# A second Fourier batch and two normalizations emitted beside the feed-forward tail, with four shared row buffers and attention sums made in place

## The chip, the core and the metric

One core of a Trainium2 chip runs the whole kernel in one launch. The metric is device time in microseconds (us). The kernel is written against a framework that owns semaphores, buffer slots and instruction order: the program *emits* instructions, each with a priority that follows the order of emission, and a planner with its own cost model then fixes one order per engine. On the chip each engine takes its instructions strictly in that order. So a line emitted later can be placed earlier by the planner if a slot and its inputs seem ready, but what happens on the chip then waits in the planner's order.

Engines: PE (TensorE, matmuls), DVE (VectorE), ACT (ScalarE), POOL (GpSimd, which also issues some DMAs), SP (issues DMAs only).

## The reference, cut to what matters

```
attn = softmax over scores q k^T / 8, only scores >= max - tau kept     # B=4, H=8, S=576, 64 per head
x    = attn @ v                                    # rows of 512
xk, xr = mixes of x and x shifted by one row (mu_k, mu_r)
x    = sigmoid(xr @ w_r) * (relu(xk @ w_k)**2 @ w_v)                    # "feed-forward", FF = 1024
X    = real(fft over rows of fft over columns)(x);   u = x + X
un   = (u - mean) / sqrt(var + 1e-6)               # per row
out  = u + relu(un @ w_ch1) @ w_ch2                # 512 -> 2048 -> 512
```

Everything is float32 in and out; matmuls use a rounded high part and a remainder (three products for each).

## The kernel before, in words

**Attention** (up to about 597 us) runs over 16 pairs of heads. `emit_av` (line 382) makes one half of a pair's output in a PSUM bank; its `post` copies the other 64 partitions to a scratch tile `avt` (one buffer, pool `at`) on ACT and adds the own half on DVE (line 401), or, for one of the four halves of a pair (bits in `AO`, `AO0`), copies both on ACT and adds on POOL (lines 398, 399). The feed-forward stream (`ffn_stream`, line 451) starts beside the second half of attention.

**Feed-forward tail** (597 to 699 us). The stream goes by batch and half: eight `kps` groups, then the previous half's transposes `xn` (`xt_out`, line 537), four `rps` groups, four `vps` groups. Each `xn` bank is copied by ACT to a tile `xnat` (line 546, one buffer in pool `ffn`) and sent to DRAM (`xd`) by a DMA that ACT issues.

**Fourier part.** For batch b: `fft_fold` (line 850) loads rows (`xa`, `xb`: one buffer each; `ra`, `rb`: tag `o` of pool `chp`, two buffers) and folds them; `fft_one` makes `G` and `H` on PE (tiles `f`, PSUM pool `pst`, two banks); `fft_two` makes `fz`, `fa` (also `pst`) and `fb`, and `make_u` adds and stores two groups `ud[2b]`, `ud[2b+1]`. Nine groups of 256 rows follow: two for each batch, and group 8 from `fft_last`.

**Normalization and mixer.** `norm(g)` loads a group (tile `un`, tag `o` as well) and normalizes it; `turn(g)` transposes it on PE (tile `ut` in the same two banks of `pst`) and copies it to `uts[g]`, a tile of pool `uta`. `uta` lies in the memory of the feed-forward pools, which `fstackp.close()` (line 1045) frees. `mixer` (line 988) then makes 36 steps (q, g), q a quarter of the weights: first q 0 and 1 for groups 0 to 3, then q 0 and 1 for groups 4 to 8, then q 2 and 3. A step has 48 `ch1` matmuls, and 24 `ch2` matmuls that run in the next step and are added by DVE to a tile `u` loaded from `ud`. `quarter(q)` converts a quarter's weights in 16 pieces (`weight_pieces`, line 45): three DVE operations (lines 67 to 69), one ACT copy, one POOL subtraction (line 73).

**What sets the order around the change.** In the loop at line 1027 each step of the stream is followed by 0.6 steps of the chain `side`. In the mixer loop at line 1059 each of a step's four yields takes 2 items of the chain `behind` up to step (0, 3), later 1.25. The last item, `done`, closes the Fourier pools and opens the later `utp`, `lnp` and `ubp` in their memory. `ahead_of` says at which mixer step `norm` and `turn` of a group are emitted.

Of the kernel before, what the change touches and what calls it, by code (L numbers as in the profile page):

```python
# [9 lines left out]
F32 = mybir.dt.float32  # L10
F32R = mybir.dt.float32r
I32 = mybir.dt.int32
ALU = mybir.AluOpType
AF = mybir.ActivationFunctionType
# [5 lines left out]
D, FF, FC = 512, 1024, 2048  # L20
HS = S // 2
NPAIR = H // 2
# [6 lines left out]
def tile_kernel(ctx: ExitStack, tc: tile.TileContext, a):  # L29
# [352 lines left out]
    def emit_av(pi, j, half):  # L382
        ps = bank([128, HS], "av")
        v, u, r = vts[pi], ptu[pi, j, half], ptr[pi, half]
        for k in range(4):
            for x in range(2):
                pe.matmul(ps, v[:, 4 * j + k, :], u[:, x, k, :], start=(k == 0 and x == 0), stop=False)  # L387
        for x in range(2):
            pe.matmul(ps, v[:, 8 + j, :], r[:, x, :], start=False, stop=(x == 1))

        def post():
            b, pr = divmod(pi, NPAIR)
            x = xunit(pi, half)
            own, oth = slice(64 * j, 64 * j + 64), slice(64 - 64 * j, 128 - 64 * j)
            tmp = at.tile([128, HS], F32, tag="avt", name="avt")
            act.activation(tmp[own], ps[oth], AF.Copy)
            if P['AO' if pi >= NPAIR else 'AO0'] >> (2 * half + j) & 1:
                act.activation(x[own, 1:], ps[own], AF.Copy)
                pool.tensor_tensor(x[own, 1:], x[own, 1:], tmp[own], op=ALU.add)
            else:  # L400
                dve.tensor_tensor(x[own, 1:], ps[own], tmp[own], op=ALU.add)
            if j == 1 and half == 1:
                dve.tensor_copy(x[:, 0:1], xT[b, pr, 0][:, HS:HS + 1])
                xdone[1] += 1
            if j == 1 and half == 0:
                xdone[0] += 1

        pending.append(post)
# [13 lines left out]
    def build_xs(b, half, which):  # L422
        fp = ffn["pool"]
        hi = fp.tile([128, 4, HS], F32R, tag="xh", name="xh")
        lo = fp.tile([128, 4, HS], F32R, tag="xl", name="xl")

        def chunk(c):
            x = xT[b, c, half]
            tmp = fp.tile([128, HS], F32, tag="xtmp", bufs=2, name="xtmp")
            m = 4 * which + c  # L430
            if P['XD'] >> (4 * which + c) & 1:
                act.activation(tmp, x[:, 0:HS], AF.Copy, scale=mus[:, 8 + m:9 + m])
                t = lo[:, c, :].bitcast(F32)
                act.activation(t, x[:, 1:], AF.Copy, scale=mus[:, m:m + 1])
                pool.tensor_tensor(tmp, t, tmp, op=ALU.add)
                act.activation(hi[:, c, :], tmp, AF.Copy)
                pool.tensor_tensor(lo[:, c, :], tmp, hi[:, c, :].bitcast(F32), op=ALU.subtract)
                return
            if b == B - 1 and P['XT'] and half + P['XT'] > 1:
                dve.tensor_scalar(tmp, x[:, 0:HS], mus[:, 8 + m:9 + m], None, op0=ALU.mult)  # L440
            else:
                pool.tensor_scalar(tmp, x[:, 0:HS], mus[:, 8 + m:9 + m], 1.0, op0=ALU.mult, op1=ALU.mult)
            dve.scalar_tensor_tensor(tmp, x[:, 1:], mus[:, m:m + 1], tmp, op0=ALU.mult, op1=ALU.add)
            act.activation(hi[:, c, :], tmp, AF.Copy)
            eng = dve if b == B - 1 and (c < P['XL']) else pool
            eng.tensor_tensor(lo[:, c, :], tmp, hi[:, c, :].bitcast(F32), op=ALU.subtract)

        builds.extend((lambda c=c: chunk(c)) for c in range(4))
        return hi, lo

    def ffn_stream():
        fp = ffn["pool"]
        xt_out = None
        for b in range(B):
            for half in range(2):
# [81 lines left out]
                def xt_out(b=b, half=half, t=t):  # L537
                    settle()
                    for t0 in (0, 128, 256):
                        tn = min(128, HS - t0)  # L540
                        ps = bank([128, D], "xn")
                        for m in range(4):
                            pe.transpose(ps[:tn, 128 * m:128 * (m + 1)], t[:, m, t0:t0 + tn], ident)

                        def post(t0=t0, tn=tn, ps=ps):
                            n = fp.tile([128, D], F32, tag="xn", name="xnat")
                            if P['XN'] >> (t0 // 128) & 1:
                                dve.tensor_scalar(n[:tn], ps[:tn], 0.5, None, op0=ALU.mult)
                            else:
                                act.activation(n[:tn], ps[:tn], AF.Copy, scale=0.5)  # L550
                            r0 = half * (HS + 1) + t0
                            act.dma_start(xd[b][r0:r0 + tn, :], n[:tn])
                            if half and t0 == 256:
                                act.dma_start(xd[b][HS:HS + 1, :], n[tn - 1:tn])

                        pending.append(post)
                        yield 0.45
                    written[b] += 1
# [170 lines left out]

    rstack = ctx.enter_context(ExitStack())  # L730
    chp = rstack.enter_context(tc.tile_pool(name="chp", bufs=1, side="right"))
    stage2 = rstack.enter_context(tc.tile_pool(name="stage2", bufs=1, side="right"))
    fstack, fstack1 = ExitStack(), ExitStack()
    psc = ctx.enter_context(tc.tile_pool(name="psc", bufs=3, space=PSUM))
# [25 lines left out]

    def load_rem(b):

        xa = chp.tile([128, D], F32, tag="o", bufs=2, name="ra")[:98]
        xb = chp.tile([128, D], F32, tag="o", bufs=2, name="rb")[:98]
        for r in (0, 33, 65):
            sp.dma_start(xa[r:r + 32], xd[b][256:288, :])
            sp.dma_start(xb[r:r + 32], xd[b][544:576, :])
        for r in (32, 97):
            sp.dma_start(xa[r:r + 1], xd[b][576:577, :])
            sp.dma_start(xb[r:r + 1], xd[b][576:577, :])  # L770
        return xa, xb
# [78 lines left out]
    def fft_fold(b):  # L850
        while written[b] < 2:
            yield
        settle()
        prs = prs_of[b] = load_pairs(b)
        ra, rb = load_rem(b)
        parts_e, parts_o = [], []
        for xa, xb in prs:
            e, o = folded(xa, xb, 128)
            yield
            parts_e.append(split_tile(e, 257, "fse"))  # L860
            parts_o.append(split_tile(o, 256, "fso"))
            yield
        e, o = folded(ra, rb, 98)
        yield
        ske = stack_tile(e, 257, "ske")
        sko = stack_tile(o, 256, "sko")
        fold_of[b] = (parts_e, parts_o, ske, sko)
        yield
# [30 lines left out]
            yield  # L899

    def fft_last():
        xa = chp.tile([128, D], F32, tag="o", bufs=2, name="xar")
        xb = chp.tile([128, D], F32, tag="o", bufs=2, name="xbr")
        for b in range(B):
            sp.dma_start(xa[32 * b:32 * b + 32], xd[b][256:288, :])
            sp.dma_start(xb[32 * b:32 * b + 32], xd[b][544:576, :])
        gr = [x.rearrange("p c b r -> p c (b r)") for x in grem]
        pa, pb = stage_2(gr[0:2], gr[2:4], 64, 0, 128)
        make_u(8, pa, pb, xa, xb)
        yield  # L910

    def chain(*gens):
        for g in gens:
            yield from g
# [4 lines left out]
    def quarter(q):  # L919

        t = [big(f"{'AB'[q % 2]}{i}", f"c{'AB'[q % 2]}{i}") for i in range(2)]
        wq[q] = t
        todo = []
        for k, src in enumerate(("w_ch1", "w_ch2")):
            to = whole([x[:, 2048 * k:2048 * k + 2048] for x in t], 2048 * q)
            todo += [(a[src], to, j) for j in range(8 * q, 8 * q + 8)]
        yield from weight_pieces(todo, None, stage2, 256, rb=4, bb=2)


    uts, hs = {}, {}  # L930

    def norm(g):

        u = [lnp.tile([128, D], F32, tag="o", bufs=2, name="un") for _ in range(2)]
        for j in range(2):
            sp.dma_start(u[j], ud[g][:, j])
        st = chp.tile([128, 32], F32, tag="lnst", bufs=1, name="lnst")
# [83 lines left out]


    fft_done, utp, lnp, ubp = False, None, chp, None
    side = chain(fft_fold(0), fft_one(0), fft_two(0))
    cgen = None
    acc = 0.0
    for _ in stream:
# [18 lines left out]
    utp = ctx.enter_context(tc.tile_pool(name="uta", bufs=1, side="left"))  # L1046
    hsp = ctx.enter_context(tc.tile_pool(name="hsp", bufs=1, side="left"))
    ubp = ctx.enter_context(tc.tile_pool(name="ub", bufs=1, side="left"))
    turn(0, norm(0))
    for _ in cgen:  # L1050
        pass
    behind = chain(
        fft_fold(1), fft_one(1), fft_two(1), quarter(1), fft_fold(2), fft_one(2), fft_two(2),
        fft_fold(3), fft_one(3), fft_two(3), fft_last(), done(),
    )

    ahead_of = {(0, 0): 1, (0, 1): 2, (0, 2): 3, (1, 2): 4, (1, 3): 5, (0, 5): 6, (0, 6): 7, (0, 7): 8}
    credit = 0.0
    for (q, g), f in mixer():
        credit += 2.0 if (q, g) < (0, 4) else 1.25  # L1060
# [141 lines left out]
```

## Time and profile before

| | us |
|---|---|
| three runs | 1182.55, 1186.1, 1186.32 (median 1186.1) |
| profiled execution | 1183.13 |
| its span, first to last instruction | 1181.4 |
| PE busy | 1054.0 (89%) |
| DVE busy | 812.3 (69%) |
| ACT busy | 596.3 (50%) |
| POOL busy | 501.2 (42%) |

Busy time of PE overlaps itself (matmuls are pipelined), so the count of matmuls in a stretch tells more than the share. A row of the view of stretches gives, for each engine, busy time and (x) the number of instructions, then PE's granted clock as a share of 2.4 GHz.

### The profile page before, as it was taken

To read this page: it belongs to the slowest core of one execution; us is meant where nothing else is said; L and a number is where in the kernel's file an instruction comes from. 1 tells how busy PE (TensorE), PEld (TensorE's weight loads), DVE (VectorE), ACT (ScalarE), POOL (GpSimd) and SP (SyncE) were. 2 spreads that over 40 slices of the span, in tenths; PEclk is the share of its full clock that TensorE was granted. 3 is DMA by queue.
4 is the path that set the end of the run, shared out by engine and by line. 5 is a ranking of instruction groups with operands and counts; after the bars stand their busy time and mean duration, and the time that the engine had idled before them with its cause. 6 is when DMAs were issued, how large, how long until landed. Compare 5 with 4: busy or idle time off the path is not lost.

```text
span 1181.4 us, 20038 instructions
## 1 busy us (share of the span) xinstructions
PE 1054.0 (89%) x7109; PEld 973.5 (82%) x7109; DVE 812.3 (69%) x2077; ACT 596.3 (50%) x1410; POOL 501.2 (42%) x649
## 2 busy tenths in 40 slices
PE   3676678899989999999979769799979999999998
PEld 3665568898989998899979758699869999999997
DVE  7999897977889887888756699536454758322222
ACT  5788777577685866858545724323232213111111
POOL 4566686656466565656442565000001536110000
PEclk9788789999999999999989889899989999999999
DMA  5333320111111111111063255434343555222221
GB/s 170 102 113 116 93 71 32 54 54 42 54 50 56 53 62 35 54 51 42 12 183 118 80 153 164 176 97 143 107 161 107 164 176 165 104 104 93 90 102 59
DMA packets 40395, 114.07 MB, mean 97 GB/s; under 512 B 6191, under 2 KB 6612, under 8 KB 40296
## 3 DMA queue, kind: packets, MB, share of 16 engines
q1 hardware_dynamic: 27200, 74.57, 19.8%
q0 software_dynamic: 10400, 33.50, 8.9%
q10 hardware_dynamic: 2696, 4.73, 1.1%
q8 instruction: 56, 0.92, 0.3%
q14 instruction: 43, 0.35, 0.1%
HBM read 84.45 MB, written 28.32 MB: 95 GB/s over the span
## 4 chain that ended last, share of the span: by engine, by line
PE 66%; DVE 16%; DMA 7%; ACT 5%; issue 4%; POOL 2%; SPq 0%; DVEq 0%; ACTq 0%; POOLq 0%
PE c1ps L972 6%; PE c1ps L971 6%; PE c1ps L973 6%; PE c2ps L984 5%; PE c2ps L985 5%; PE c2ps L986 5%; PE av L387 4%; PE s L212 4%; PE t L320 3%; DMA rawqk<-in_qk 3%; DVE q L167 2%; PE vps L526 2%; PE kps L418 2%; DVE small L252 2%; PE vps L528 2%
## 5 line engine op out<-in xcount | busy, mean ns | idle before, releaser
L977 DVE SCALAR_TENSOR_TENSOR hl<-c1ps,hh 128x256 fp32r<-128x256 f32 x144 | 60.9, 423 | 185.0 <-ACT hh L976 184.3
L976 ACT ACTIVATE hh<-c1ps 128x256 fp32r<-128x256 f32 x144 | 55.2, 383 | 230.6 <-PE c1ps L973 230.1
L1009 POOL DMA_DIRECT2D ud<-u x54 | 29.5, 547 | 255.0 <-DVE u L1008 199.2
L252 DVE TENSOR_REDUCE small<-s 128x1 f32<-128x576 f32 x144 | 106.3, 749 | 15.2 <-PE s L212 12.2
L267 DVE SCALAR_TENSOR_TENSOR e<-s,small,e 128x576 f32<-128x576 f32 x128 | 102.1, 811 | 9.3 <-ACT e L263 7.4
L273 POOL TENSOR_SCALAR e<-e,small 128x576 f32<-128x576 f32 x104 | 82.4, 798 | 43.0 <-DVE small L633 33.7
L263 ACT ACTIVATE e<-s,small 128x576 f32<-128x576 f32 x128 | 92.6, 743 | 12.5 <-DVE small L252 9.1
L320 PE MATMUL t<-ident,e 128*128 128x128 f32 x512 | 84.1, 294 | 15.1 <-DVE ptr L306 6.4
L971 PE MATMUL c1ps<-ut,cA 128*128 128x256 f32 x288 | 83.2, 291 | 14.4 <-ACT ut L962 14.4
L212 PE MATMUL s<-kh,q 128*128 128x288 f32 x256 | 66.0, 342 | 26.1 <-DVE q L167 13.6
L972 PE MATMUL c1ps<-ut,cA 128*128 128x256 f32 x288 | 83.6, 290 | 1.1 <-DVE ut L963 1.1
L306 DVE TENSOR_TENSOR pt<-t,pt 128x512 fp32r<-128x512 f32 x100 | 67.8, 684 | 23.5 <-ACT pt L305 22.9
L973 PE MATMUL c1ps<-ut,cA 128*128 128x256 f32 x288 | 82.9, 288 | 0.0
L320 PEld LDWEIGHTS t<-ident,e 128*128 128x128 f32 x512 | 65.6, 151 | 20.4 <-ACT e L639 6.0
L418 PE MATMUL kps<-xh,wk 128*128 128x288 f32 x256 | 79.3, 310 | 2.2 <-ACT relu L473 1.6
L971 PE MATMUL c1ps<-ut,cB 128*128 128x256 f32 x288 | 81.2, 282 | 0.0
L973 PE MATMUL c1ps<-ut,cB 128*128 128x256 f32 x288 | 81.1, 281 | 0.0
L972 PE MATMUL c1ps<-ut,cB 128*128 128x256 f32 x288 | 81.0, 281 | 0.0
L387 PE MATMUL av<-pt,v 128*128 128x288 f32 x408 | 72.8, 311 | 7.4 <-ACT pt L305 4.0
L488 POOL TENSOR_TENSOR k<-relu,k 128x288 fp32r<-128x288 f32 x64 | 56.7, 887 | 51.6 <-ACT k L486 51.3
L419 PE MATMUL kps<-xl,wk 128*128 128x288 f32 x256 | 77.5, 303 | 0.0
L420 PE MATMUL kps<-xh,wk 128*128 128x288 f32 x256 | 77.2, 302 | 0.0
(243 smaller groups left out, 3607.1 us busy)
## 6 DMA issues: line engine op xcount, KB each, us to landing
rawqk<-in_qk SPq DMA_DIRECT2D x32, 608.0 KB
u<-ud SPq DMA_DIRECT2D x36, 512.0 KB
wraw<-in_w_ch POOLq DMA_DIRECT2D x64, 256.0 KB, 3.0
ud<-u POOLq DMA_DIRECT2D x54, 256.0 KB, 2.5
rawv<-in_v SPq DMA_DIRECT2D x16, 288.0 KB
un<-ud SPq DMA_DIRECT2D x18, 256.0 KB
out<-u SPq DMA_DIRECT2D x18, 256.0 KB
wraw<-in_w_k SPq DMA_DIRECT2D x8, 512.0 KB
```

Of the source, the lines that this page charges most:

```text
L212: pe.matmul(ps[:, h, 0:HS], q[:, c:c + 128], kk[:, h * HS:(h + 1) * HS], start=(x == 0), stop=(x == 1),)
L252: dve.tensor_reduce(st[:, 0:1], sps[n][:, :, 0:HS], axis=AX.XY, op=ALU.max, negate=True)
L263: act.activation(two(eview(n)), sps[n][:, :, 0:HS], AF.Exp, bias=st[:, 0:1])
L267: dve.scalar_tensor_tensor(e, sps[n][:, :, 0:HS], st[:, 1:2], e, op0=ALU.is_ge, op1=ALU.mult, accum_out=st[:, 2:3])
L273: pool.tensor_scalar(e, e, st[:, 2:3], 1.0, op0=ALU.mult, op1=ALU.mult)
L320: pe.transpose(t[:, k, :], e[:, o + 128 * k:o + 128 * (k + 1)], ident)
L387: pe.matmul(ps, v[:, 4 * j + k, :], u[:, x, k, :], start=(k == 0 and x == 0), stop=False)
L418: pe.matmul(ps, wh, x[0][:, k, :], start=(k == 0), stop=False)
L419: pe.matmul(ps, wh, x[1][:, k, :], start=False, stop=False)
L971: pe.matmul(ps, wh, ut[0][:, k, :], start=(k == 0), stop=False)
L972: pe.matmul(ps, wh, ut[1][:, k, :], start=False, stop=False)
L973: pe.matmul(ps, wl, ut[0][:, k, :], start=False, stop=(k == 3))
```

## The change

`emit_av` copies the other half straight into the result tile with ACT and adds in place on DVE, in all cases; `avt` and the POOL form are gone. From the opening of `chp` on, `xnat` is allocated there, with tag `o`, which now has four buffers (also used by `ra`, `rb`, `xar`, `xbr` and, while `norm` uses `chp`, by `un`). The weight stage has three raw buffers in place of four. `side` now also holds batch 1's fold, `norm(0)` and `norm(1)`, and batch 1's two stages. `turn(0)` and `turn(1)` stand together before the mixer. `behind` no longer has batch 1, and groups 2 and 3 are normalized one step earlier.

```diff
@@ emit_av / post
-            tmp = at.tile([128, HS], F32, tag="avt", name="avt")
-            act.activation(tmp[own], ps[oth], AF.Copy)
-            if P['AO' if pi >= NPAIR else 'AO0'] >> (2 * half + j) & 1:
-                act.activation(x[own, 1:], ps[own], AF.Copy)
-                pool.tensor_tensor(x[own, 1:], x[own, 1:], tmp[own], op=ALU.add)
-            else:
-                dve.tensor_tensor(x[own, 1:], ps[own], tmp[own], op=ALU.add)
+            act.activation(x[own, 1:], ps[oth], AF.Copy)
+            dve.tensor_tensor(x[own, 1:], ps[own], x[own, 1:], op=ALU.add)
@@ ffn_stream / xt_out
-                            n = fp.tile([128, D], F32, tag="xn", name="xnat")
+                            n = fp.tile([128, D], F32, tag="xn", name="xnat") if last is None else last.tile([128, D], F32, tag="o", bufs=4, name="xnat")
@@ after chp is opened
+    last = chp
@@ load_rem (and fft_last likewise)
-        xa = chp.tile([128, D], F32, tag="o", bufs=2, name="ra")[:98]
-        xb = chp.tile([128, D], F32, tag="o", bufs=2, name="rb")[:98]
+        xa = chp.tile([128, D], F32, tag="o", bufs=4, name="ra")[:98]
+        xb = chp.tile([128, D], F32, tag="o", bufs=4, name="rb")[:98]
@@ quarter
-        yield from weight_pieces(todo, None, stage2, 256, rb=4, bb=2)
+        yield from weight_pieces(todo, None, stage2, 256, rb=3, bb=2)
@@ norm
-        u = [lnp.tile([128, D], F32, tag="o", bufs=2, name="un") for _ in range(2)]
+        u = [lnp.tile([128, D], F32, tag="o", bufs=4 if lnp is chp else 2, name="un") for _ in range(2)]
@@ before the stream's tail
-    side = chain(fft_fold(0), fft_one(0), fft_two(0))
+    normed = {}
+    def norms():
+        for g in range(2):
+            normed[g] = norm(g)
+            yield
+    side = chain(fft_fold(0), fft_one(0), fft_two(0), fft_fold(1), norms(), fft_one(1), fft_two(1))
@@ before the mixer
-    turn(0, norm(0))
+    for g in range(2):
+        turn(g, normed[g])
     behind = chain(
-        fft_fold(1), fft_one(1), fft_two(1), quarter(1), fft_fold(2), fft_one(2), fft_two(2),
+        quarter(1), fft_fold(2), fft_one(2), fft_two(2),
         fft_fold(3), fft_one(3), fft_two(3), fft_last(), done(),
     )
-    ahead_of = {(0, 0): 1, (0, 1): 2, (0, 2): 3, (1, 2): 4, (1, 3): 5, (0, 5): 6, (0, 6): 7, (0, 7): 8}
+    ahead_of = {(0, 0): 2, (0, 1): 3, (1, 2): 4, (1, 3): 5, (0, 5): 6, (0, 6): 7, (0, 7): 8}
```

## Rows read from the trace of the kernel before

**Rows 1.** Stretches: length, busy (count) of PE, PEld, DVE, ACT, POOL, PEclk, DMA.

```profile
664.00:699.20 35.20, 26.66 (x174) 24.65 (x172) 32.85 (x65) 15.97 (x37) 24.29 (x36) 0.85 0.42 117
...
710.00:753.40 43.40, 36.54 (x228) 31.96 (x229) 35.02 (x86) 16.79 (x47) 17.14 (x27) 0.93 0.62 201
753.40:854.00 100.60, 99.54 (x645) 89.92 (x646) 53.05 (x146) 31.94 (x90) 5.42 (x10) 0.96 0.31 106
...
870.40:1164.00 293.60, 293.58 (x1888) 267.69 (x1889) 130.51 (x282) 60.46 (x151) 58.49 (x94) 0.99 0.34 115
```

**Rows 2.** Timeline of PE: start, length, line, tiles, idle before and its releaser.

```profile
671.07 0.61 PE L418 MATMUL rps<-xh,wr 128*128 128x288 f32 x1 [3.48 <-ACT xnat L550]
...
676.50 0.61 PE L418 MATMUL rps<-xh,wr 128*128 128x288 f32 x1 [2.05 <-ACT xnat L550]
...
698.57 0.61 PE L543 MATMUL xn<-ident,tg 128*32 128x128 f32 x4 [0.25 <-ACT xnat L550]
...
710.04 0.80 PE L971 MATMUL c1ps<-ut,cA 128*128 128x256 f32 x2 [10.87 <-ACT ut L962]
...
749.15 1.36 PE L960 MATMUL ut<-ident,un 128*128 128x128 f32 x8 [3.45 <-ACT un L952]
753.40 0.80 PE L971 MATMUL c1ps<-ut,cA 128*128 128x256 f32 x2 [2.89 <-ACT ut L962]
```

**Rows 3.** Chain that ended last, 697 to 711 us: start, length, what.

```profile
702.37 3.40 DMA xd<-xnat
...
706.46 2.37 DMA xd<-xnat
...
708.91 0.61 ACT ut L962
```

**Rows 4.** Timeline of PE: who holds the two `pst` banks.

```profile
652.47 0.66 PE L960 MATMUL ut<-ident,un 128*128 128x128 f32 x4
...
715.35 0.38 PE L802 MATMUL f<-tc,fseh 128*128 128x290 f32 x1
```

**Rows 5.** DVE groups by line and form, 714 to 742.5 us: count, busy, mean ns.

```profile
L838 DVE TENSOR_TENSOR xa<-xa,fdd 128x257 f32<-128x257 f32 x2 | 0.8, 420 | 0.0
...
L810 DVE TENSOR_TENSOR G<-f,G 128x290 fp32r<-128x290 f32 x2 | 0.9, 446 | 0.0
```

**Rows 6.** Timelines of DVE and POOL: two-input DVE operations with and without POOL's beside them.

```profile
608.05 1.85 DVE L780 TENSOR_TENSOR fy<-fp,fq 128x257 f32<-128x257 f32 x1
...
608.06 1.55 POOL L488 TENSOR_TENSOR k<-relu,k 128x288 fp32r<-128x288 f32 x2
...
683.94 1.22 DVE L69 SCALAR_TENSOR_TENSOR wbits<-wraw,wbits 128x256 int32<-128x256 int32 x1
...
684.12 0.76 POOL L73 TENSOR_TENSOR cA<-wbits,cA 128x256 fp32r<-128x256 f32 x1
...
734.66 0.42 DVE L69 SCALAR_TENSOR_TENSOR wbits<-wraw,wbits 128x256 int32<-128x256 int32 x1
```

**Rows 7.** Timeline of SP: loads of batches 2 and 3, and the first `u` after them.

```profile
745.45 0.80 SPq L757 DMA_DIRECT2D xa<-xd  x2
...
766.71 0.32 SPq L766 DMA_DIRECT2D ra<-xd  x1
...
804.98 0.80 SPq L757 DMA_DIRECT2D xa<-xd  x2
```

**Rows 8.** Chain that ended last, 840 to 872 us.

```profile
853.32 4.92 DMA u<-ud
...
870.42 0.79 PE c1ps L971 x2
```

**Rows 9.** Attention's sums: durations min/median/max of POOL's form; and the first table load.

```profile
L399 POOL TENSOR_TENSOR xt<-xt,avt x16: 792/802/1260, 72.1 to 595.6; 64x288 f32<-64x288 f32 x16
...
597.61 0.74 POOL L746 DMA_DIRECT2D tc<-in_tc  x1 [1.25 <-DVE xt L401]
```

**Rows 10.** The page's DMA issues: KB each, us from issue to landing.

```profile
wraw<-in_w_ch POOLq DMA_DIRECT2D x64, 256.0 KB, 3.0
```

More of the change, by code (lines that the diff above doesn't have):

```diff
@@ L449, in build_xs @@
         return hi, lo
+    last = None
     def ffn_stream():
@@ L901, in fft_last @@
     def fft_last():
-        xa = chp.tile([128, D], F32, tag="o", bufs=2, name="xar")
-        xb = chp.tile([128, D], F32, tag="o", bufs=2, name="xbr")
+        xa = chp.tile([128, D], F32, tag="o", bufs=4, name="xar")
+        xb = chp.tile([128, D], F32, tag="o", bufs=4, name="xbr")
         for b in range(B):
```

## The prediction

> **What bounds the kernel now.** I read first the page's table of 40 slices (attention up to about 597 us, DVE the fullest engine in its first part; then a broken stretch in which PE's clock falls several times; from about 870 us PE full to the end), then a view by stretches, then PE's waits inside the broken stretch, then the chain of waits.
>
> From 870.4 to 1164 us PE does 1888 matmuls in 293.6 us [rows 1]. A mixer step is 48 + 24 = 72 matmuls, so that is 26 steps (1872) and 16 transposes: 293.6 / 26 = 11.3 us a step, with no wait. Step 9 of 36, (0, 5), starts at 870.42 [rows 8]; from there to the end the kernel is bound by PE and the change alters nothing. So the question is only: **when does step 9 start?** Everything earlier in it is gained one for one.
>
> Before that, three holes. (1) The last feed-forward matmuls end at 699.2 (698.57 + 0.61), the first of the mixer starts at 710.04 after 10.87 us of idle [rows 2]. The chain says why: the last `xnat` copies share one buffer, two DMAs of 3.40 and 2.37 us stand in series, and only behind the second does ACT copy `ut`, at 708.91 [rows 3]: `xnat` lies in a pool whose memory `ut` takes over. (2) The same buffer holds PE back by 3.48 and 2.05 us at 671 and 676.5 [rows 2]. (3) PE transposed group 0 at 652.47 already, and those tiles sat in both `pst` banks until ACT could copy them at 708.91; so batch 1's `f` started only at 715.35 [rows 3, 4]. Its 68 matmuls then shared 710 to 753.4 with two mixer steps, and group 2, which needs them, kept PE waiting 3.45 and 2.89 us at 749 and 753 [rows 1, 2].
>
> Behind this stands a second chain, batches 2 and 3. Their buffers are single, so batch 2 loads at 745.45, batch 3 at 804.98 [rows 7], and only when the last store is issued does SP load `u` into the memory that `done` freed: 853.32, landing 4.92 us later; step 9 starts 17.1 us after that load [rows 8]. Before, both chains arrive together at 853.
>
> **The change, part by part.**
>
> *`xnat` in four buffers.* Takes away the serial DMAs: `ut` can be copied when the last transposes are done, 699.2, not 708.91 [rows 2, 3]: -9.7 us. In the tail it takes away 2.05 us; of the 3.48 I count 1, since `xs` of that half is still being built. Sum -3. Against it: `un` of groups 0 and 1 hold up to four `o` buffers, so the third `xnat` of a half can wait until group 0 is transposed. If so ACT stands with it and PE's banks stay full: between 0 and about +10 us; I take 0, since by order of emission two `xnat` stand ahead of `un(1)`, and keep 10 in the range.
>
> *Batch 1's two stages beside the tail.* What really moves is `fft_one(1)` and `fft_two(1)`; the planner had the fold ahead already. PE: 68 matmuls of 256 to 290 columns; a mixer step of 11.3 us streams 48 x 256 + 24 x 512 = 24,576 columns [rows 1], 0.46 ns each, so I estimate 0.125 us a matmul and 8.5 us in all. In 664 to 699.2 PE has 174 matmuls in 35.2 us [rows 1]; at 0.13 us each that is 23 us, so some 12 us are free, 3 of which I have just spent. I charge 4 of the 8.5 to the tail (between 0 and 8.5). DVE: 5 splits of 0.45 and 12 adds of 0.42 us [rows 5] = 7.3 us, in a stretch where DVE is busy 32.85 of 35.2 us [rows 1] with weight pieces. Those are not needed before the mixer reads them, so they slip behind, into the mixer's first steps, where DVE was busy 35.0 of 43.4 us (710 to 753.4). Tail and mixer start: 699.2 - 3 + 4 = 700.2, then one transposition, copy and first matmul, 2 to 3 us: **703** in place of 710.
>
> DVE's two-input operations take 0.42 us with POOL quiet, but 1.22 when POOL's subtraction of 0.76 lies inside, and 1.85 beside two of POOL's of together 1.55 [rows 6]. Eight of the moved adds have two inputs in SBUF, and before they ran with POOL quiet. Between 0 and 8 x 0.76 = 6 us more for DVE; I take 3, as not every add meets one. The Trainium skill (SBUF — State Buffer, "Who interferes with whom") says that a DVE instruction with two SBUF inputs and a GpSimd instruction that reads SBUF exclude each other for the whole instruction; by it all that overlap pay in full, which speaks against this move and would put 6 in place of 3; the trace's 1.85 us agrees.
>
> *The mixer's first nine steps.* 710 to 753.4 held two steps, 8.5 us of batch 1 and 6.3 us of waits for it: 43.4 - 8.5 - 6.3 = 28.6 us. 753.4 to 854 held seven steps with batches 2 and 3 beside them, 100.6 us [rows 1]. PE alone would then start step 9 at 703 + 28.6 + 100.6 = **832**.
>
> *Batches 2 and 3.* `xa` is free when batch 1 is stored: I put its last adds at 695 to 698 and the load at 703, not 745.45 [rows 7]: -42. Batch 2's `ra` waited for an `o` buffer until 766.71 [rows 7], 21 us behind `xa`; with four buffers some 8 us of that go. DVE is fuller at 703 to 745 than at 745 to 790: +7 (between 0 and 15). `u` is loaded at 853.3 - 42 - 8 + 7 = 810.
>
> *An earlier `done`.* `behind` loses 11 items, 51 to 40. Of these 32 are emitted in the first 16 yields, the rest at 1.25: `done` falls on yield 16 + 7 = 23 (step 5), before on 16 + 16 = 32 (step 7). So `u` of step 5, not of step 7, is the first to lie in the freed memory, and PE stands two steps earlier if the batches are late. With 17.1 us from that load to a step's start, as before, it is now step 8 that starts at 810 + 17 = 827, and step 9 at **838**.
>
> *In-place sums.* 16 of POOL's adds of 0.80 us [rows 9] become DVE adds of about 0.46, and 16 ACT copies go. PE is the fuller engine in the later attention; in the early part DVE is, with 4 or 5 of the 16: between -1 and +2, I take 0. The first table load waited for the last reader of `avt` until 597.61 [rows 9]; without `avt` it can go 2 us sooner, which the tail hides.
>
> *Three raw buffers.* With two loads ahead and 3.0 us from issue to landing [rows 10] a piece may go every 1.5 us without waiting for a load; DVE needs 3 x 0.42 = 1.3 us for one, and 0.8 more where POOL's subtraction lies inside [rows 6]: 0. If loads slow down, quarter 1 is late, but is needed only at step 4, near 750.
>
> *Sum.* Step 9 at the later of 832 and 838: 838, so 870.4 - 838 = 32 us gained: span 1181.4 - 32 = 1149, profiled execution 1183.1 - 32 = 1151. The median of the runs shown, 1186.1, is 3 above that execution, and one run lies below it; I add 1: **1152**.
>
> **The rivals.**
>
> *B. Group 0 takes the banks again.* If PE has `ut(0)` in both `pst` banks before `f` of batch 1, as at 652 [rows 4], batch 1 waits for the pool, about 702, and not 715: it runs beside steps 0 and 1. Loads of batch 2 at 735, `u` at 853 - 10 - 8 + 2 = 837, step 9 at 837 + 28 = 865: 1177. For it: the planner did so. Against: `f` is now emitted far ahead of `ut`, and its first input comes with the first half of the fold.
>
> *C. Slower, by the earlier `done`.* If batches 2 and 3 end no sooner than now, PE stands at step 7 waiting for `u`, with the same 17 us behind it: step 9 at 853 + 28 = 881, 11 us late: 1194. It decides from a load of `u` at 842 on (842 + 28 = 870). For it: `quarter(1)` is now emitted ahead of batch 2 and DVE is full there. Against: that needs batch 2 to lose all of 42 us.
>
> *D. The gain is used up.* The tail pays for batch 1 in full (8.5 PE, 13 DVE with `xnat` held): start near 712 and, through late stores, step 9 at 868 to 872: 1183. The change then does not do what it says, since the work stood beside nothing idle.
>
> **How the numbers follow.** Forecast A 0.57 at 1152, on its own from 1138 to 1166: both chains 10 to 14 us better (832 - 8 for PE, `u` at 797), or the 10 of `xnat` and the upper 8 on DVE. B 0.20 at 1177, C 0.12 at 1194, D 0.11 at 1183. A measurement of this kernel tells about 0.3%, 3.6 us: 1182.5 to 1189.7 is no change. Faster: A, 0.17 of B and 0.03 of D: 0.77. Same: 0.03 of B and 0.08 of D: 0.11. Slower: C, 0.12. The range from 1138 to 1182 leaves out C, half of D and a few in a hundred below.
>
> **What would show it.** The idle before the first `c1ps` falls from 10.87 to under 4 us and stands near 700; `f` of batch 1 on PE lies between 650 and 690, ahead of `ut`; no PE wait near 749; `u` loaded into freed memory near 810; step 9 near 838, then 11.3 us a step unchanged. Wrong would be: `ut` ahead of `f`; ACT waiting for an `o` buffer in the tail; PE standing at step 7 for `u` longer than about 10 us; or attention's end moved by more than 3 us.

## The result

The changed kernel takes 1139.1 us (median of four runs, 1136.3 to 1142.4) where the kernel before takes 1184.3 beside it: a ratio of 0.962, 95% interval 0.9585 to 0.9656. The forecast of 1152 had the sign right and a gain too small: 32 us at step 9, where 44.7 came. The time lies at the lower edge of the stated range (1138 to 1182), and one of the four runs below it.

In the profiled execution step 9 starts at 825.7 us in place of 870.4, and the span falls from 1181.4 to 1138.1. The view of stretches of the changed kernel, columns as in [rows 1]: the last 35 us of the feed-forward, mixer steps 0 and 1, steps 2 to 8, steps 9 to 34.

```profile
660.00:695.10 35.10, 29.09 (x202) 25.90 (x200) 29.74 (x80) 19.11 (x46) 16.62 (x26) 0.96 0.53 162
696.60:725.50 28.90, 27.08 (x152) 23.08 (x153) 23.14 (x67) 12.59 (x31) 12.82 (x21) 0.89 0.62 201
725.50:825.70 100.20, 100.20 (x669) 90.47 (x668) 67.94 (x184) 34.58 (x96) 21.55 (x37) 1.00 0.51 170
825.70:1120.80 295.10, 295.10 (x1908) 268.40 (x1907) 132.71 (x276) 59.53 (x151) 59.54 (x98) 1.00 0.36 123
```

From 725.5 on the view shows PE without a gap. Behind step 9 little has changed: 295.1 us for 26 steps, where [rows 1] has 293.6. PE's timeline holds these waits where before had those of [rows 2], and no other over 0.6 us between 665 and 826:

```profile
685.87 0.40 PE L523 MATMUL vps<-k,wv 128*128 128x288 f32 x1 [1.86 <-DVE tg L529]
...
692.89 2.20 PE L540 MATMUL xn<-ident,tg 128*128 128x128 f32 x9 [2.55 <-DVE tg L529]
...
696.62 0.58 PE L969 MATMUL c1ps<-ut,cA 128*128 128x256 f32 x1 [1.54 <-ACT ut L960]
```

The 10.87 us ahead of the mixer are 1.54; the `xnat` waits are gone and waits for DVE's `tg` have taken part of their place. Batch 1's first `f` runs on PE at 643.18 (before 715.35 [rows 4]), ahead of group 0's transposes:

```profile
643.18 0.30 PE L800 MATMUL f<-tc,fseh 128*128 128x290 f32 x1
...
668.38 0.63 PE L958 MATMUL ut<-ident,un 128*128 128x128 f32 x4 [0.53 <-DVE fdd L835]
```

SP's timeline, which answers to [rows 7] and the first row of [rows 8]: batch 2's rows load at 677.69 (before 745.45), and `u` goes into freed memory at 786.46, ahead of the last store of the Fourier part at 803.66:

```profile
677.69 0.80 SPq L755 DMA_DIRECT2D xa<-xd  x2
...
786.46 0.32 SPq L996 DMA_DIRECT2D u<-ud  x1
786.82 0.90 SPq L934 DMA_DIRECT2D un<-ud  x2
...
803.66 0.38 SPq L844 DMA_DIRECT2D ud<-xbr  x1
```

**Where the 44.7 us at step 9 come from**, by the two traces. The attention ends 3.5 us earlier (first `vps` at 592.0 for 595.5). The stretch from there to the last `vps` takes 97.3 us for 100.1: -2.8. From the last `vps` to the last `xn` it takes 5.8 for 3.6: +2.2, the `tg` waits. The idle time ahead of the first mixer matmul: -9.3. Steps 0 to 8: 129.1 for 160.4, -31.3. Sum -44.7; 1.4 of it are lost again behind step 9.

### The profile page after: what moved, and what is told of

The parts are those of the page before. It is cut to its first block, busy times and chain, and to the rows that moved or that the text cites. A ratio compares the mean times of both kernels' runs of the same rounds, so it can differ in the third digit from the quotient of the medians.

```text
span 1138.1 us, 19981 instructions
## 1 busy us (share of the span) xinstructions
PE 1038.4 (91%) x7109; PEld 960.0 (84%) x7109; DVE 806.7 (71%) x2093; ACT 588.9 (52%) x1396; POOL 483.8 (43%) x633
## 4 chain that ended last, share of the span: by engine, by line
PE 65%; DVE 16%; ACT 7%; DMA 6%; issue 4%; POOL 2%; SPq 0%; DVEq 0%; ACTq 0%; POOLq 0%
PE c1ps L969 6%; PE c1ps L971 6%; PE c1ps L970 6%; PE c2ps L984 6%; PE c2ps L982 6%; PE c2ps L983 6%; PE av L387 3%; PE s L212 3%; DVE q L167 3%; DMA rawqk<-in_qk 2%; PE t L320 2%; DVE small L252 2%; PE kps L413 2%; DVE e L267 2%; PE kps L415 2%
## 5 line engine op out<-in xcount | busy, mean ns | idle before, releaser
L267 DVE SCALAR_TENSOR_TENSOR e<-s,small,e 128x576 f32<-128x576 f32 x128 | 102.4, 811 | 7.3 <-ACT e L263 5.6
L320 PE MATMUL t<-ident,e 128*128 128x128 f32 x512 | 81.2, 290 | 7.9 <-DVE ptr L306 2.9
L969 PE MATMUL c1ps<-ut,cA 128*128 128x256 f32 x288 | 82.5, 286 | 2.2 <-ACT ut L960 1.5
L970 PE MATMUL c1ps<-ut,cA 128*128 128x256 f32 x288 | 82.0, 285 | 0.0
L523 PE MATMUL vps<-k,wv 128*128 128x288 f32 x256 | 76.7, 302 | 5.4 <-DVE tg L529 4.6
L971 PE MATMUL c1ps<-ut,cA 128*128 128x256 f32 x288 | 81.6, 283 | 0.0
L485 POOL TENSOR_TENSOR k<-relu,k 128x288 fp32r<-128x288 f32 x64 | 54.1, 847 | 60.6 <-ACT k L483 59.7
L413 PE MATMUL kps<-xh,wk 128*128 128x288 f32 x256 | 78.3, 306 | 0.8 <-ACT relu L470 0.4
L415 PE MATMUL kps<-xh,wk 128*128 128x288 f32 x256 | 75.6, 296 | 0.0
```

What stands on the lines that cost most here:

```text
L267: dve.scalar_tensor_tensor(e, sps[n][:, :, 0:HS], st[:, 1:2], e, op0=ALU.is_ge, op1=ALU.mult, accum_out=st[:, 2:3])
L320: pe.transpose(t[:, k, :], e[:, o + 128 * k:o + 128 * (k + 1)], ident)
L413: pe.matmul(ps, wh, x[0][:, k, :], start=(k == 0), stop=False)
L415: pe.matmul(ps, wl, x[0][:, k, :], start=False, stop=(k == nk - 1))
L969: pe.matmul(ps, wh, ut[0][:, k, :], start=(k == 0), stop=False)
L970: pe.matmul(ps, wh, ut[1][:, k, :], start=False, stop=False)
```

## The experiments

The table has what the sections below speak of: in each profiled execution the start of step 0, step 2 and step 9, the difference of the last two, and the ratio to the kernel before on the same chip.

| kernel | step 0 | step 2 | step 9 | 2 to 9 | ratio (95%) |
|---|---|---|---|---|---|
| before | 710.0 | 753.4 | 870.4 | 117.0 | 1 |
| + four buffers (e8) | 716.7 | 765.6 | 868.0 | 102.4 | 0.9998 (0.9979 to 1.0016) |
| + buffers, group 0 early (e10) | 702.5 | 768.4 | 870.6 | 102.2 | 0.9986 (0.9970 to 1.0002) |
| + buffers, sums (e2) | 708.7 | 757.7 | 858.8 | 101.1 | 0.9910 (0.9883 to 0.9937) |
| + buffers, sums, group 0 early (e9) | 692.1 | 754.6 | 856.0 | 101.4 | 0.9883 (0.9860 to 0.9907) |
| + buffers, sums, groups 0, 1 early (e12) | 690.2 | 746.7 | 850.3 | 103.6 | 0.9875 (0.9854 to 0.9896) |
| changed kernel (a0: again) | 696.6 | 725.5 | 825.7 | 100.2 | 0.9609 (0.9586 to 0.9632) |
| changed, `xnat` alone in its buffer (e1) | 706.3 | 733.6 | 835.6 | 102.0 | 0.9689 (0.9661 to 0.9717) |
| changed, old sums (e3) | 703.2 | 730.1 | 832.4 | 102.3 | 0.9677 (0.9653 to 0.9701) |
| changed, scratch tile, DVE adds (e4) | 707.8 | 735.3 | 835.4 | 100.1 | 0.9727 (0.9712 to 0.9743) |
| changed, `u` over the last tables (e5) | 697.0 | 725.2 | 833.1 | 107.9 | 0.9637 (0.9616 to 0.9658) |
| changed, subtraction on DVE (e6) | 695.2 | 721.6 | 821.7 | 100.1 | 0.9604 (0.9586 to 0.9623) |

**a0: the changed kernel beside the others.**

> The changed kernel itself, on the same chip as the three edits beside it: 1139 us, within 0.3% (1136 to 1143).

1138.6 us (1137.8 to 1140.1). The differences below are from this. The kernels ran on three chips, on which the kernel before took 1182.5 to 1185.1 us, so between chips the ratios of the table decide.

**e1: `xnat` back in its one buffer.**

```diff
- n = last.tile([128, D], F32, tag="o", bufs=4, name="xnat")
+ n = fp.tile([128, D], F32, tag="xn", name="xnat")
```

> The changed kernel with xnat back in its single buffer in the feed-forward pool; all else stays. Theory 1 (from the mixer's start PE is the bound, so a later start is paid one for one): the idle before the first c1ps is again about 10 us, the feed-forward waits of 2 to 4 us come back, and the time is 10 to 13 us longer, 1149 to 1152. Rival (batches 2 and 3 set when step 9 starts, as the prediction had it): the gap comes back but is hidden, 0 to 3 us, 1139 to 1142.

1147.9 us, 9.4 above, a little under the 10 to 13 of Theory 1. The mixer starts 9.7 us later, at 706.3, and from there to step 9 nothing differs (129.3 us for 129.1). In PE's timeline the wait of [rows 2] is back, and in the chain that ended last (start, length, what) the two stores in series of [rows 3]:

```profile
706.30 0.79 PE L969 MATMUL c1ps<-ut,cA 128*128 128x256 f32 x2 [9.50 <-ACT ut L960]
```

```profile
699.25 2.69 DMA xd<-xnat
...
702.64 2.46 DMA xd<-xnat
...
705.17 1.09 ACT ut L960 x2
```

So what `xnat` in the shared buffers is worth in the changed kernel is shown, and it is two of the prediction's terms: the idle ahead of the mixer is 8.0 us longer (9.50 for 1.54; the prediction took 9.7), and the feed-forward from the attention's end to the last `xn` 3.7 longer (106.8 us for 103.1; the prediction took 3). That their sum at the mixer's start is again 9.7 is chance: the attention ended 2.0 us earlier in this run.

**e8: the four buffers alone, in the kernel before** (with three raw weight buffers, as in the change).

```diff
- n = fp.tile([128, D], F32, tag="xn", name="xnat")
+ n = last.tile([128, D], F32, tag="o", bufs=4, name="xnat")   # ra, rb, xar, xbr, un: bufs=4 too
```

> The kernel before with the buffers alone: xnat in chp, four o buffers, three raw buffers. Theory 1: the mixer and batch 1 both start some 10 us earlier and all of it is kept, 1171 to 1175. Rival (batches 2 and 3 hold step 9 at the end of step 8): 1181 to 1184, the earlier start turns into a longer wait near step 8.

1184.5 us: no change. The rival's time came, to half a microsecond, but not its wait near step 8. The stores are no longer waited for; PE's timeline has a longer wait in their place, for the normalized rows of group 0. SP's timeline shows when they were loaded, and SP's waits (who waited for what: us in total, times, longest) what stood ahead of them:

```profile
714.10 1.97 PE L963 MATMUL ut<-ident,un 128*128 128x128 f32 x8 [18.65 <-ACT un L955]
```

```profile
696.00 0.44 SPq L939 DMA_DIRECT2D un<-ud  x1
696.49 0.43 SPq L1001 DMA_DIRECT2D u<-ud  x1
697.48 0.32 SPq L939 DMA_DIRECT2D un<-ud  x1
```

```profile
SPq L1001 <- PE xn L545: 50.9, 1, 50.9
...
SPq L939 <- DMA xd<-xnat: 0.5, 1, 0.5
```

Group 0's `un` stands behind the three `xnat` of the last half in the order of emission, and now in the same four buffers: it is loaded at 696 to 697.5 us, where before it had two buffers without `xnat` and its transposes ran at 652.47 [rows 4]. On SP the first of its two loads stands behind a load of `u`, for which SP waits 50.9 us until the last `xn`; only the second waits for a store of `xnat`, 0.5 us. The buffers are all that differs from the kernel before, so the planner's new order on SP comes of them; how it arrives at that order no run takes apart. In exchange steps 2 to 8 run without the waits that [rows 8] ends in: 102.4 us for 117.0. The mixer starts 6.7 us later and reaches step 2 12.2 later; 14.6 less behind it leave step 9 at 868.0.

**e2: batch 1 and both normalizations late, buffers and sums as changed.**

```diff
- side = chain(fft_fold(0), fft_one(0), fft_two(0), fft_fold(1), norms(), fft_one(1), fft_two(1))
+ side = chain(fft_fold(0), fft_one(0), fft_two(0))
  # turn(0, norm(0)), behind and ahead_of as in the kernel before
```

> The changed kernel with batch 1's fold and stages, norm and turn of groups 0 to 3 emitted where they were; the four shared buffers, the three raw buffers and the sums stay. Theory 1: batch 1's 8.5 us of PE and the waits of some 6 us for group 2 come back into the first steps, and done falls late again: 15 to 28 us longer, 1154 to 1167. Rival (the buffers alone bring the gain): 1139 to 1143.

1174.1 us, 35.5 above, more than Theory 1 asked for: e8's wait is in it, 18.74 us here. In the chain that ended last, group 0's second load comes behind a store of `xnat` and takes 8.86 us:

```profile
686.70 2.70 DMA xd<-xnat
689.47 8.86 DMA un<-ud
```

**e9 and e10: group 0's normalization early, batch 1 late**, in the changed kernel and in e8.

```diff
  def norms():
-     for g in range(2):
-         normed[g] = norm(g)
-         yield
+     normed[0] = norm(0)
+     yield
- side = chain(fft_fold(0), fft_one(0), fft_two(0), fft_fold(1), norms(), fft_one(1), fft_two(1))
+ side = chain(fft_fold(0), fft_one(0), fft_two(0), norms())
```

> The changed kernel with batch 1's transform and group 1's normalization put back to where they were before, but group 0's normalization kept beside the last feed-forward halves. With group 0 also late the time was 1174 us, 35.5 above the changed kernel, and PE waited 18.7 us before the first transposition of group 0, since its load queued behind the stores of the x rows, whose four buffers it shares. Theory 1, of these 35.5 some 16 are that wait, and 15 to 24 are batch 1's work in the first nine steps: mixer start at 689 to 693, steps 0 to 9 in 150 to 158 us as in the two kernels with batch 1 late (150.1 and 151.3), 1154 to 1162. Rival 1, batch 1's place is worth little and nearly all was the wait: 1140 to 1148. Rival 2, the transform of three batches holds step 9 at the same instant however early the mixer starts: step 9 at 856 to 860, 1170 to 1175.

> The kernel before with the x rows in the shared four buffers (as in the run with the buffers alone, 1184.5) and group 0's normalization moved beside the last feed-forward halves; batch 1 stays late, sums as before. Theory 1, the buffers alone gained nothing because they took away 10.9 us ahead of the first mixer product and put in 18.7 ahead of the first transposition, since group 0's load queues behind the x rows in the same buffers; with that normalization early the mixer starts at 696 to 699 (before 710.0), steps 0 to 9 take 151 to 160 us and the time is 1160 to 1172. Rival, the transforms of batches 1 to 3 hold step 9 at 868 to 870 whatever the mixer's start: 1181 to 1186.

1172.7 and 1183.5 us. Theory 1 fell in both. The mixer does start at 692.1 and 702.5, 16.6 and 14.2 us earlier than without the edit, but step 9 moves by 2.8 us, and by 2.6 the wrong way. What the mixer wins at its start it stands at step 2, the first that needs rows of batch 1. The waits in e9, from PE's timeline:

```profile
713.82 1.87 PE L958 MATMUL ut<-ident,un 128*128 128x128 f32 x8 [4.48 <-ACT un L950]
717.14 0.61 PE L800 MATMUL f<-tc,fseh 128*128 128x290 f32 x1 [1.44 <-DVE ut L961]
...
748.52 1.97 PE L958 MATMUL ut<-ident,un 128*128 128x128 f32 x8 [8.48 <-ACT un L950]
754.60 0.80 PE L969 MATMUL c1ps<-ut,cA 128*128 128x256 f32 x2 [4.12 <-ACT ut L960]
```

and its stretches, from the last `xn` to step 2 and from there to step 9:

```profile
689.70:754.60 64.90, 40.91 (x228) 34.52 (x228) 50.53 (x123) 23.06 (x59) 25.42 (x40) 0.84 0.60 194
754.60:856.00 101.40, 100.88 (x655) 90.99 (x656) 56.80 (x160) 34.91 (x97) 5.40 (x10) 0.96 0.38 123
```

24.0 us idle in the first, 0.5 in the second. The rival's time (in e9 the second rival's) was right and its mechanism not quite: not the transforms of three batches hold step 9, but batch 1's holds step 2, and from step 2 on PE is full.

**e12: only batch 1 late**, groups 0 and 1 early.

```diff
- side = chain(fft_fold(0), fft_one(0), fft_two(0), fft_fold(1), norms(), fft_one(1), fft_two(1))
+ side = chain(fft_fold(0), fft_one(0), fft_two(0), norms())
  # behind begins with fft_fold(1), fft_one(1), fft_two(1); ahead_of {(0, 1): 2, (0, 2): 3, ...}
```

> The changed kernel with only batch 1's transform put back behind the mixer's first steps; groups 0 and 1 are both normalized beside the last feed-forward halves (both hold rows of batch 0 only). In the three kernels with batch 1 late whose rows I followed, step 2 comes 37.5 to 38.7 us after the first table product f of batch 1 (before 715.35 to 753.4, with group 0's normalization alone early 717.1 to 754.6, the same with the sums of before 729.7 to 768.4), and step 9 another 101 to 102 us after step 2 where the four buffers are shared. And f stands on PE behind the transposition of group 1, whose rows were loaded only at 698 to 709, behind the x rows in the same buffers. Theory 1: with group 1 early, f follows the mixer's start (about 692) by 0 to 8 us, step 2 comes at 730 to 738, step 9 at 832 to 840 (825.7 in the changed kernel), 1145 to 1153; so most of the 34 us between 1138.6 and 1172.7 are group 1's normalization and not batch 1's place. Rival: batch 1's fold is what is late, f stays at about 717, step 9 at 856, 1168 to 1174.

1167.5 us: a miss. `f` came at 697.46, as Theory 1 said, but step 2 followed 49 us behind it, not 38, at 746.7; PE did steps 0 and 1 and then stood for rows stored at 729.3 to 732.6:

```profile
744.05 1.97 PE L958 MATMUL ut<-ident,un 128*128 128x128 f32 x8 [17.30 <-ACT un L950]
```

So emitting batch 1 early, with all else as changed, is worth 0.9875 - 0.9609 = 0.0266 of 1185, 31 us, and 24.6 us at step 9 in the two profiled executions. But batch 1 is later in e12 than it was in the kernel before. There the planner had put batch 1's fold beside the tail, as the prediction says, and its remainder rows `ra` were loaded at 653.19 us; in e12 they come at 694.17, on SP behind a `u` again, and then behind an `xnat`, whose buffers they share. SP's timeline before and in e12, and SP's waits in e12:

```profile
653.19 1.25 SPq L766 DMA_DIRECT2D ra<-xd  x3
```

```profile
694.17 0.32 SPq L764 DMA_DIRECT2D ra<-xd  x1
```

```profile
SPq L996 <- PE xn L540: 52.5, 1, 52.5
SPq L764 <- DMA xd<-xnat: 4.8, 1, 4.8
```

In e8, e2, e9 and e10 `ra` comes as late, at 690 to 702 us. So with the four buffers the late batch 1 comes later still, and its early emission takes that back too; no run prices the two apart, and why step 2 followed `f` by 49 us in place of 38 wasn't isolated. Between the last `xn` and step 2 PE stands idle 21.4 us here, 24.0 in e9, 17.7 in the kernel before (54.2 less 36.5) and 3.3 in the changed kernel (30.4 less 27.1, 695.1 to 725.5). Whether e12 and e9 differ the intervals don't tell.

**e3 and e4: the attention's sums.** e3 has the old ones, e4 the scratch tile with DVE doing every addition.

```diff
- act.activation(x[own, 1:], ps[oth], AF.Copy)
- dve.tensor_tensor(x[own, 1:], ps[own], x[own, 1:], op=ALU.add)
+ tmp = at.tile([128, HS], F32, tag="avt", name="avt")
+ act.activation(tmp[own], ps[oth], AF.Copy)
+ dve.tensor_tensor(x[own, 1:], ps[own], tmp[own], op=ALU.add)
```

> The changed kernel with the attention's sums as they were before: the scratch tile avt, and the POOL addition for some of them. In the kernel with the buffers alone the attention's 138th step starts at 557.6 us, in the one that also has the in-place sums at 551.5 (before 557.4): the only difference between those two is the sums. Theory 1, the in-place sums are the 6 us: the attention ends 4 to 6 us later and the time is 4 to 7 us above the changed kernel's 1138.6. Rival, the order of the work differs between the versions by chance and the sums cost nothing themselves: within 1.5 us of it, and the attention's end moves with no relation to the sums.

> The changed kernel with the scratch tile of the attention's sums back, but with VectorE doing every addition, where the run with the old sums (1146.5, 8 us above the changed kernel) had both the scratch tile and POOL for one in eight. Theory 1, the POOL form is the cost (two-input work of POOL beside VectorE's, and one more ScalarE copy): within 2 us of 1138.6. Rival, the scratch tile is the cost (its buffer must be added before the next half's copy may be written): 1143 to 1148.

1146.5 us for e3, 8.0 above the changed kernel, and 1150.2 for e4, by ratio 0.0118 of 1185, 14 us: above both expected ranges, in both runs. e8 and e2 differ by the sums alone as well: 10 us. The last product of the attention starts (row of a group: minimum, median, maximum ns, first and last start) in the changed kernel and in e4 at

```profile
L389 PE MATMUL av<-ptr,v x102: 288/296/401, 165.1 to 590.9; 128*128 128x288 f32 x102
```

```profile
L389 PE MATMUL av<-ptr,v x102: 288/295/382, 167.7 to 599.2; 128*128 128x288 f32 x102
```

The seven traced kernels with in-place sums lie between 588.8 and 592.1 there, the five with the scratch tile between 594.4 and 599.2, though the order of PE's work differs among them. So with the scratch tile the attention ends 2 to 10 us later, and POOL's share of the adds is not the cause: e4, without it, is no faster than e3. How it costs them stays open. The waits straight at the tile are small: in e4 ACT's copies wait 1.4 us for DVE's adds. The difference appears at the transposes of `e`, where PE waits 15.1 us in the kernel before and 7.9 in the changed one, and these have nothing to do with `avt`. The tile may alter the order in which the framework places the attention's instructions, or its buffer may delay a few of them that others follow; a version with two scratch buffers wasn't tried.

**e5: `u` in other memory.** The three late pools are opened in the opposite order, so that `u` lies over the tables in use until the last store.

```diff
- utp, lnp, ubp opened in this order
+ ubp, lnp, utp opened in this order
```

> The changed kernel with the three late pools opened in the opposite order, so that the residual rows u lie in the memory of the tables that live until batch 3's last store, and the transposed rows in that of the first stage's tables. Theory 1, memory comes free piece by piece, and my bound 'u can only be loaded behind the last store' failed because u lay over the first stage's memory (u(5) loaded at 786.46, right behind the first stage's last matmul, the last store at 803.7): here u(5) loads at about 804, the normalization's load of group 4 queues behind it on SP (786.83 before), its chain of some 12 us ends at 819 instead of 800, and step 8, at 813.4 now, waits: 4 to 10 us above 1138.6, step 9 at 830 to 836. Rival, the loads move but nothing waits for them, since group 5 is used only after step 9: within 1.5 us.

1143.0 us, 4.5 above; by ratio 3.3 us, with intervals that overlap, so the time alone doesn't settle it. The trace does: `u` is loaded at 802.20 in place of 786.46, behind the last store:

```profile
801.26 0.42 SPq L844 DMA_DIRECT2D ud<-xbr  x1
802.20 0.32 SPq L996 DMA_DIRECT2D u<-ud  x1
802.58 0.92 SPq L934 DMA_DIRECT2D un<-ud  x2
```

Step 8 starts 15.9 us behind that load, at 818.1, step 9 at 833.1. So memory comes free piece by piece, not with the pool's closing, and which piece `u` gets is worth 7.4 us at step 9 (two profiled executions of the changed kernel have 825.7 and 825.9), of which some come back behind it.

**e6: the subtraction of the weights' low halves on DVE** for the first two quarters.

```diff
- pool.tensor_tensor(l, wf, h.bitcast(F32), op=ALU.subtract)
+ (dve if ahead and src[0][2] < 16 else pool).tensor_tensor(l, wf, h.bitcast(F32), op=ALU.subtract)
```

> The changed kernel with the subtraction of the mixer weights' low halves on VectorE instead of POOL for the first two quarters. In the last 10 us before the mixer PE waits 1.86, 0.46 and 2.55 us for the tg product on VectorE, and there wbits steps of 0.42 us take 1.1 to 1.3 where POOL subtracts at the same time. Theory 1, the two engines hold each other up: without POOL's subtraction the long wbits steps go back to 0.42 us, the tg waits shrink by 3 to 5 us and the time is 1133 to 1137. Rival, VectorE is simply full there (29.7 of 35.1 us busy): 32 more operations of 0.3 us each lengthen its queue, 1139 to 1147.

1135.5 us, ratio 0.9604 beside 0.9609: not told apart from the changed kernel. What it does to DVE is plain. In the changed kernel the wait of 2.55 us above has this in DVE's timeline, and this in POOL's:

```profile
691.37 1.10 DVE L68 SCALAR_TENSOR_TENSOR wbits<-wraw,wbits 128x256 int32<-128x256 int32 x1
692.39 0.44 DVE L529 SCALAR_TENSOR_TENSOR tg<-tg,vps 128x288 f32<-128x288 f32 x1
```

```profile
691.44 0.73 POOL L73 TENSOR_TENSOR cA<-wbits,cA 128x256 fp32r<-128x256 f32 x1
```

DVE's step of 0.42 us lasts 1.10, by about the length of POOL's subtraction, and `tg` stands behind it. With the subtraction on DVE the group over 659 to 694 us is

```profile
L68 DVE SCALAR_TENSOR_TENSOR wbits<-wraw,wbits x12: 396/420/426, 659.9 to 692.7; 128x256 int32<-128x256 int32 x12
```

where the changed kernel had a maximum of 1312 ns; the subtraction itself takes 420 ns on DVE for 747 on POOL. The `tg` waits ahead of the mixer shrink from 4.9 to 2.5 us, less than the 3 to 5 expected, and the tail gains nothing by it: the mixer starts 1.4 us earlier, but the attention had ended 1.3 earlier (first `vps` at 590.7 for 592.0), and a wait of 1.44 us ahead of an `rps` is new.

## Why the prediction was right, and where not

**Steps 0 to 8: right to the tenth, the second part by luck.** 28.6 + 100.6 = 129.2 us were forecast; 28.9 + 100.2 = 129.1 came. Taking the batch's matmuls and its waits out of the first stretch held. Leaving the second as it was hid two errors that cancel. The 100.6 us hold 645 matmuls [rows 1], the changed kernel's 100.2 hold 669: in the kernel before some 30 came only behind 854. And PE's granted clock in them was 0.96, since it stood at its lower level, 1.2 GHz, in the first 7.8 us, behind the waits of 3.45 and 2.89 us [rows 2]; in the changed kernel it is 1.00 throughout. The view of stretches of the kernel before:

```profile
753.40:761.20 7.80, 6.74 (x27) 6.25 (x28) 6.96 (x23) 2.61 (x8) 0.00 (x0) 0.50 0.37 131
...
854.00:870.40 16.40, 9.47 (x33) 6.74 (x31) 7.35 (x21) 2.92 (x5) 2.16 (x4) 0.79 0.91 298
```

An estimate: 100.6 us at 0.96 are 96.6 at full clock, and 24 matmuls more at the changed kernel's 0.15 us each are 3.6: 100.2. The prediction had no term for either.

**The start of the mixer: 703 forecast, 696.6 measured.** Three terms were off. Attention's end was taken as unmoved and is 3.5 us earlier, more than the 3 us that the prediction named as a sign of being wrong: "between -1 and +2, I take 0" priced the adds themselves, and e3, e4, e2 and e8 put the sums at 8 to 14 us of the whole time. The tail up to the last `xn` was charged +1 net and came out at -0.6, with less for batch 1 and 2.2 for `tg`. The last step was 1.5 us, not 2.8. 3.5 + 1.6 + 1.3 = 6.4. The -9.7 for the buffer is 9.3 between the two traces and 8.0 in e1.

**Batches 2 and 3: the step that failed.** I put their chain at 838 and made it the bound; it never bound. Batch 2 loaded at 677.7, not 703, since `f` went far ahead of the tail's end, but `ra`, for which the prediction wanted less than the 21 us of before, followed only at 715.6, 38 us behind, so the last store, at 803.7, was just 6 us ahead of the 810 I gave for the load behind it. What decided was another assumption: that `u` gets memory only behind the last store. It got that of the first stage's tables, at 786.5, behind batch 3's last `f`. In e5, where `u` has to wait for the last store, my sum nearly comes true: the load at 802, step 8 at 818 (15.9 us behind; I took 17.1), step 9 at 833. So the 6 us from 832 to 838 fell away: 6.4 + 6 = 12.4, the whole distance from 838 to 825.7.

**What each part is worth.** The prediction gave the buffer 9.7 us as if it stood alone. Alone it is worth nothing (e8), since group 0's load then comes behind the `xnat` of the same buffers, and batch 1's `ra` too: the "third `xnat`" that I feared would wait for `un` was the right coupling in the wrong direction. It counts once the normalizations and batch 1 are moved (e1). Moving the normalizations counts little without batch 1 (e9, e10, e12). Emitting batch 1 early is the largest part, 25 to 31 us (e12), with the four buffers in place. The parts aren't additive.

**The rivals.** B didn't come: `f` at 643 is 25 us ahead of the first transpose of group 0. C didn't: PE never stands at step 7 for `u`. D didn't; its fear, that DVE's queue eats the gain, is the 2.2 us at `tg`. Mutual blocking of DVE and POOL, for which I took 3 us on the moved adds, showed in the weight steps: 3 long ones of 11 at line 68 in the tail, about 2.4 us more, and e6 takes them away without a gain in time that can be told.

## What to carry to other kernels

When a consumer starts before its producer's rows are stored, ask at which of its steps it first runs out: starting it earlier is worth nothing up to there (e9), and moving the producer is worth the whole hole. Before tiles of two stages share a ring of buffers, list who takes it in the order of emission; a load that was free to go early can come behind the stores of the other stage. And look up which piece of memory a late tile gets before putting its load behind the last user of the pool.

## What the runs showed of the hardware

A DVE step with two inputs in SBUF went from 0.42 to between 1.1 and 1.3 us with one POOL subtraction of some 0.75 us beside it, and in e6's tail none took over 0.58. The Trainium skill (SBUF — State Buffer, "Who interferes with whom") names the exclusion. The traces agree, with 0.7 to 0.9 us more a step, though in the rows above DVE's step is recorded as the first to start (691.37 against 691.44) and is still the one that is lengthened. Two steps at line 67, which have one input and take 0.28 us otherwise, took 0.82 and 0.85 beside the same subtraction, so in these traces not only steps with two inputs are lengthened. Loads of some 3 us took 7 to 9 us when `u`, `un`, weights and `ra` were asked for within some 10 us: `un` 8.86 us in e2, where a later `un` took 2.88, and a piece of weights (3.0 us in [rows 10]) in e8's chain that ended last

```profile
696.06 6.94 DMA wraw<-in_w_ch
```

Where PE stood idle longer its granted clock was mostly lower. From the last `xn` to step 2 it was 0.75 to 0.85 of full speed (a mean of its two levels, 1.2 and 2.4 GHz) in the kernels with batch 1 late, where PE stood idle 18 to 31 us (0.84 with 24.0 us in e9's row above), and 0.88 in the changed kernel with 3.3 us idle; behind step 2 it was 1.00 there.
